# A token tile kept aside and paired with one of a later batch, with other sums for the last softmax

## The chip, the cores and the metric

The kernel runs on one core of a Trainium2 chip. Five engines work side by side, each through its own instructions in order: TensorE (PE; its weight loads PEld), VectorE (DVE), ScalarE (ACT), GpSimd (POOL) and SyncE (SP), which here only issues transfers. The metric is the device time of one execution in microseconds.

## What is computed

Attention with normalised queries and keys, and behind it a two-layer network with a leaky ReLU on all tokens:

```python
q_n, k_n = (rmsnorm(q, g_q), rmsnorm(k, g_k))      # q, k, v: (8, 12, 448, 64)
scores = scale * np.matmul(q_n, k_n.transpose(0, 1, 3, 2))
scores = scores - np.max(scores, axis=-1, keepdims=True)
attn = np.exp(scores)
attn = attn / (np.sum(attn, axis=-1, keepdims=True) + 1e-09)
attn_out = np.matmul(attn, v)
x = attn_out.transpose(0, 2, 1, 3).reshape(3584, 768)
h = x @ w_in                                       # (768, 2048)
out = np.maximum(0.01 * h, h) @ w_out              # (2048, 768)
```

## The kernel before

**Units.** The attention is cut into 24 units `u` of four heads; three units make a batch `b`. A unit computes seven score blocks in four steps `d` (1, 2, 2 and 2 blocks, `STEPS`), through two PSUM slots `sT`; ACT turns each block into exponentials `et` (line 214). At `d == 0` the maximum is formed on DVE (`shift_max`, L232 and L234), a matmul spreads it over the partitions (`shift_mm`, L244), and DVE makes the bias `eb` from it; in the same place PE does the last unit's value products (`pv`, L340) and its softmax sums. For units 4 and up the sums are formed in four column tiles (`zcol`, L283, 128x224): Ln and Exp on 224 columns (L300, L305), four transfers that broadcast the result (`rz`, L310, on SP), a copy of the values out of PSUM (L295), and a multiplication on POOL or, for the last unit, on DVE (L320). The first units use `zsum_slot`, `pv`, `zinv` and `xmul` instead: ones matmuls that leave the sums already spread (L265), Ln and Exp on 896 columns (L326, L327), and a multiplication straight out of PSUM (L349).

**The network as filler.** `push(b)` puts batch `b`'s network into a queue of items, each with a cost in microseconds; `fill(u, d, jobs)` takes items out behind every score step, in proportion to the time that is left (weights `WD`), and puts one of the small `jobs` (loads, squares, sums, norms of later units) behind each. Batch `b` is pushed at unit 3b+3, step 3. Work that an item leaves for DVE, ACT or a queue goes to `pend` (`later`) and is put out by `flush` at the start of the next item or at the end of the fill. What is left after the last unit, three items, covers the last softmax; then batch 7 follows alone.

**First layer.** `moe1(b, ft)` makes one block of 128 of the 2048 hidden features for all 448 tokens with six matmuls and a Prelu on ACT into `gt` (L362, L356). Batches 6 and 7 (`late`) use a seven-product scheme instead (`late1`, L564): for a pair of feature blocks `s`, items `(n, s)` are products of 224 columns, six matmuls each, combined by DVE (L577, L612) before the Prelu (L574). Batch 6 does it for two of four pairs (`LATE_HALF`, in which "M" is a plain `moe1`), batch 7 for all. The operands are sums of weights (`win_sum`, L533) and of tokens (`x_sum`, L550).

**Second layer.** `gt` holds 512 token columns of a pair of batches; `col(t)` gives the place of token tile `t` (0 to 6, 128 tokens). Tiles 0 to 2 belong to the even batch; the odd one overwrites columns 64 to 511. A tile alone is four items of eight matmuls of 128x384 (`moe2`, L403). Two tiles together take seven items of eight (`seven`, L444) with operand sums `sa` from `s1` to `s4` on DVE (L425 to L434). In even batches from 2 on, tile 2 goes alone and 0 and 1 together; in odd ones (3, 4) and (5, 6).

**Banks.** Four PSUM banks serve all these products (`aux`). From batch 6's first `late1` item on, `hold` takes all four and a free list hands them out first in, first out; `drop` returns a bank.

Of the kernel before, what the change touches and what calls it, by code (L numbers as in the profile page):

```python
# [18 lines left out]
def kernel(  # L19
# [44 lines left out]
            banks = [psum.tile([P, 512], FP32, tag="aux", bufs=4, name=f"bank{i}") for i in range(4)]  # L64
            held.append(banks)

    def drop(bank):
        if held:
            held[0].append(bank)

    ident16 = cst.tile([P, P], FP16)
    make_identity(nc, ident16)
# [40 lines left out]
    def rows(x, u):  # L113
        b, g = divmod(u, NQ)
        return x[b, QH * g:QH * g + QH].rearrange("(a r) (p t) d -> (r p) a (t d)", r=2, t=NS)

    def load(u, engines=None):
        raw[u] = [raws.tile([P, 2, NS, D], FP32, tag=name, name=name) for name in ("rq", "rk")]
        st[u] = {}
        for t, src, eng in zip(raw[u], (q, k), engines or (nc.sync, nc.sync)):  # L120
            eng.dma_start(t.rearrange("p a t d -> p a (t d)"), rows(src, u))
# [12 lines left out]
    def buf(u, name):  # L134
        if name not in st[u]:
            shape, dtype, bufs = SHAPES[name]
            st[u][name] = prep_p.tile(shape, dtype, tag=name[:2] if bufs == 3 and name != "qkT" else name, bufs=bufs, name=name)
        return st[u][name]

    BOTH = (0, 1)  # L140
# [171 lines left out]
    def xmul_sb(u):  # L312
        xmul_pool(u, nc.vector)
# [44 lines left out]
    def moe1(b, ft):  # L358
        xt = xts[b]
        hps = aux([P, 512], FP32, "hps")  # L360
        for kt in range(KT):
            nc.tensor.matmul(hps[:, 0:S], win16[:, kt // 2, kt % 2, ts(ft, P)], xt[:, kt // 2, kt % 2],  # L362
                             start=(kt == 0), stop=(kt == KT - 1))
        prelu(b, gt[:, ft, 64 * (b % 2):64 * (b % 2) + S], hps[:, 0:S])
        drop(hps)

    def moe1_part(b, banks, k0, k1):
        for ft in range(2):
# [46 lines left out]
    def weight_sum(n, x):  # L415
# [2 lines left out]
                (wblock(1, 1), wblock(0, 1)), (wblock(1, 0), tw[:, 1]))[n]  # L418
        nc.vector.tensor_tensor(tw[:, n, x], a[:, x], b[:, x], op=ALU.subtract)

    def gblock(t, j):
        return gt[:, HF * j:HF * j + HF, ds(col(t), P)]

    def s1(tt, x=slice(0, 8)):
# [14 lines left out]
    def seven(pair, tt, nxt=None, last=False):  # L439
        g = {}  # L440

        def mm(bank, a, b, first):
            for f in range(HF):
                nc.tensor.matmul(bank[:, 0:HC], a[:, f], b[:, f], start=(first and f == 0), stop=(f == HF - 1), skip_group_check=not first)  # L444

        def bank(name):
            g[name] = aux([P, 512], FP32, name)
            return g[name]

        def add(dst, src, name):  # L450
            nc.vector.tensor_tensor(dst, g[name][:, 0:HC], src, op=ALU.add)

        def put(i, c):
            store(pair, tt[i], g["o"][i], c, last)

        def i0():
            flush()
            g["o"] = (out_tile(), out_tile())
            mm(bank("ma"), gblock(tt[0], 0), wblock(0, 0), True)
            later(lambda: nc.vector.tensor_copy(g["o"][1][:, L], g["ma"][:, 0:HC]))  # L460

        def i1():
            flush()
            mm(bank("mb"), sa[:, 1], tw[:, 1], True)
            later(lambda: add(g["o"][1][:, L], g["o"][1][:, L], "mb"))
            later(lambda: drop(g["mb"]))

        def i2():
            flush()
            mm(g["ma"], gblock(tt[0], 1), wblock(1, 0), False)  # L470
            later(lambda: nc.scalar.copy(g["o"][0][:, L], g["ma"][:, 0:HC]))
            later(lambda: drop(g["ma"]))
            if last:
                later(put, 0, L)

        def i3():
            flush()
            mm(bank("mc"), sa[:, 0], tw[:, 0], True)
            later(lambda: add(g["o"][1][:, R], g["o"][1][:, L], "mc"))
            if nxt:  # L480
                later(s1, nxt)

        def i4():
            flush()
            mm(bank("md"), sa[:, 2], tw[:, 2], True)
            later(lambda: add(g["o"][1][:, R], g["o"][1][:, R], "md"))
            if last:
                later(put, 1, R)

        def i5():  # L490
            flush()
            mm(g["mc"], sa[:, 3], wblock(1, 1), False)
            if nxt:
                later(s2, nxt)
            later(lambda: add(g["o"][0][:, R], g["o"][1][:, L], "mc"))
            later(lambda: drop(g["mc"]))
            later(put, 0, R if last else LR)
            if nxt:
                later(s3, nxt)
                later(s4, nxt)  # L500

        def i6():
# [35 lines left out]

    def x_tiles():
        if not xs:  # L540
            two = [prep_p.tile([P, 2, HK, HX], FP16, tag="sq", bufs=3, name="xs") for i in range(2)]
            for n in range(1, 5):
                xs[n] = two[n // 3][:, (n - 1) % 2].rearrange("p k (t x) -> p k t x", t=NS)

# [7 lines left out]
    def late1(b, tail, after):  # L552
# [36 lines left out]
        def start():  # L589
            hold()  # L590
            if tail:
                for i in range(2):
                    drop(slot()[:, 0])
            for name in ("u", "v"):
                if name not in tmp:
                    tmp[name] = raws.tile([P, 2, S], FP32, tag="rq" if name == "u" else "rk", name=name)

        def item(n, s):
            flush()
# [28 lines left out]
            for fn in after.get((n, s), ()):  # L628
                pend.append(fn)

        return item

    LATE_ALL = ((1, 0), (2, 0), (7, 0), (1, 1), (6, 0), (7, 1), (1, 2), (5, 0), (4, 0), (6, 1), (3, 0), (2, 1), (7, 2), (5, 1),
                (4, 1), (6, 2), (3, 1), (1, 3), (7, 3), (5, 2), (4, 2), (6, 3), (3, 2), (2, 2), (5, 3), (4, 3), (2, 3), (3, 3))
# [1 line left out]
                 (2, 3), (5, 3), (4, 3), "M", (3, 3))  # L636

    queue = []

    def also(fn, *more):  # L640
        def both():
# [5 lines left out]
    def push(b):  # L647
        pair, odd = divmod(b, 2)
        fast = b > 0
        order = [f // 2 + HF * (f % 2) for f in range(FT)] if odd else range(FT)  # L650
        items = [(1.13, lambda ft=ft: (flush(), moe1(b, ft))) for ft in order]
        half = [(slice(0, 4)), (slice(4, 8))]
        late = b >= LATE
# [1 line left out]
        if late:  # L655
            if odd:
                tt = (3, 4)
                for ns, f in (((1, 3), s1), ((4, 2), s2), ((3, 2), s3), ((5, 3), s4)):
                    after[ns] = [lambda f=f: f(tt, half[0])]
                after[3, 3] = [lambda f=f: f(tt, half[1]) for f in (s1, s2)]  # L660
            else:
                after[6, 2] = [lambda: win_sum(1, 0, (raws, "rq", 3))]
                after[1, 3] = [lambda: win_sum(2, 0, (raws, "rk", 3))]
                after[5, 2] = [lambda: win_sum(4, 0, (prep_p, "n16", 1))]
            item = late1(b, odd, after)
            fts = [0, 8, 1, 9, 2, 10, 3, 11]
            items = []
            for w in (LATE_ALL if odd else LATE_HALF):
                if w == "M":
                    items.append((1.13, lambda ft=fts.pop(0): (flush(), moe1(b, ft))))  # L670
                else:
                    items.append((0.575, lambda w=w: item(*w)))
        if odd:
            tt, tn = (3, 4), (5, 6)
            items += [(1.31, fn) for fn in seven(pair, tt, tn)]
            for n, x, fs in ((len(items) - 7, 1, (s3, s4)),) if late else ((8, 0, (s1, s2)), (10, 0, (s3, s4)), (FT - 1, 1, (s1, s2)), (FT, 1, (s3, s4))):
# [3 lines left out]
        else:  # L680
            tiles = (2,) if fast else (0, 1, 2)
            std = [lambda t=t, h=h, p=p: moe2(pair, t, h, p) for t in tiles for h in range(2) for p in range(2)]
            if fast:
                tt = (0, 1)
                std[0] = also(std[0], lambda: later(s1, tt), *[lambda: later(win_sum, 3, 0)] * late)
                std[1] = also(std[1], lambda: later(s2, tt))
                std[2] = also(std[2], lambda: later(s3, tt), lambda: later(s4, tt))
                std += seven(pair, tt)
# [55 lines left out]
    with tc.manual_schedule():  # L744
# [182 lines left out]
        for u in range(3, NU):  # L927
            for d in range(4):
# [67 lines left out]
                if d == 2 and 6 <= u < 8:  # L996
                    job(xmul_sb, u - 1)
                if u == NU - 2 and d == 0:
                    for n, tile_ in ((1, (raws, "rq", 3)), (2, (raws, "rk", 3)), (3, None), (4, (prep_p, "sq", 3))):
                        job(win_sum, n, 1, tile_)  # L1000
                    for n in (3, 1, 2, 4):
                        job(x_sum, LATE, n)
# [1 line left out]
                    for ti in range(2):  # L1004
                        job(prep_sq, u + 3, ALL, (ti,))
                fill(u, d, jobs)
        zcol(NU - 1)
        zcol_ln(NU - 1)
        zcol_inv(NU - 1)
        pv_slot(NU - 1)  # L1010
        pv_out(NU - 1)
        for i, fns in enumerate(([lambda: xmul_sb(NU - 1)], [lambda n=n: x_sum(B - 1, n) for n in (3, 1)], [lambda n=n: x_sum(B - 1, n) for n in (2, 4)])):
            c, fn = queue[i]
            queue[i] = (c, also(fn, *[lambda f=f: later(f) for f in fns]))
        push(B - 1)
        while queue:
            queue.pop(0)[1]()
# [29 lines left out]
```

## Time and profile before

| | us |
|---|---|
| median of 3 runs | 422.75 |
| lowest and highest | 422.69, 425.65 |
| the profiled execution | 425.65 |
| its span, first to last instruction | 423.8 |
| PE busy, weight loads | 404.8, 223.4 |
| ACT busy | 303.6 |
| DVE busy | 272.4 |
| POOL busy | 82.9 |
| chain that ended last: PE, ACT, DVE | 71%, 14%, 8% |

The spans are those of one profiled execution, which is also the slowest of the three runs. PE's busy time is that of its pipeline: a stall shorter than a matmul's flight doesn't show as idle. Units 5 to 21 take between 13.0 and 16.8 us each, unit 22 takes 18.8 and unit 23 17.6 us (from one maximum to the next, and to the last unit's sums). The last unit's sums start at 374.66 us, batch 7's first layer at 380.81 and its second layer at 401.04.

### The profile page before, as it was taken

Reading aid. Unit: us, or ns where it says so; the run is one execution under the profiler, and the core shown is the slowest. Engines: PE = TensorE matmul, PEld = TensorE weight load, DVE = VectorE, ACT = ScalarE, POOL = GpSimd, SP = SyncE. Lnnn points to the kernel's source line nnn. Section 1 sums busy time; section 2 is a strip of 40 time slices with the busy share of each in tenths; the row PEclk is TensorE's granted clock in tenths of the full one; section 3 lists DMA queues with packets and bytes.
Section 4 is the critical chain, followed back from the end, with each engine's and each line's share of the span. In section 5 each row is a group of like instructions: output and inputs, shape, how many; then the busy total and the mean of one; then the engine's idle time right before and its main releaser. Section 6 shows DMA issues by size and latency. Waiting matters only on the chain.

```text
span 423.8 us, 9575 instructions
## 1 busy us (share of the span) xinstructions
PE 404.8 (96%) x3959; PEld 223.4 (53%) x3959; DVE 272.4 (64%) x439; ACT 303.6 (72%) x475; POOL 82.9 (20%) x75
## 2 busy tenths in 40 slices
PE   7787999999999999999999999999999999998996
PEld 6454454544445544555445545555445557557963
DVE  5888674886668736665458736565448779416762
ACT  5999877778886599777887689767887476633600
POOL 1967432200020211210210211210220110010000
PEclk9999999999999999999999999999999999998999
DMA  7999997899555885668564896678532550232013
GB/s 265 216 251 252 240 251 110 210 159 209 142 152 97 216 230 88 162 180 175 142 153 78 208 208 132 159 179 172 153 67 47 137 142 2 48 76 77 2 47 104
DMA packets 72527, 62.88 MB, mean 148 GB/s; under 512 B 36388, under 2 KB 67620, under 8 KB 72484
## 3 DMA queue, kind: packets, MB, share of 16 engines
q1 hardware_dynamic: 61888, 50.08, 46.3%
q0 software_dynamic: 10272, 11.80, 17.8%
q8 instruction: 31, 0.51, 0.5%
q10 hardware_dynamic: 324, 0.39, 0.3%
q14 instruction: 12, 0.10, 0.1%
HBM read 45.61 MB, written 11.01 MB: 134 GB/s over the span
## 4 chain that ended last, share of the span: by engine, by line
PE 71%; ACT 14%; DVE 8%; issue 3%; DMA 2%; SPq 1%; DVEq 0%; ACTq 0%
PE hps L362 23%; ACT et L214 8%; PE sT L195 7%; PE sT L340 5%; PE ma L444 5%; PE md L444 5%; PE bank L564 4%; PE mc L444 4%; PE bank L444 4%; PE op L403 3%; PE zc L283 3%; PE mb L444 3%; DVE n L167 2%; ACT gt L356 2%; PE sT L444 2%
## 5 line engine op out<-in xcount | busy, mean ns | idle before, releaser
L214 ACT ACTIVATE et<-sT,eb 128x896 f16<-128x896 f32 x166 | 159.6, 1011 | 18.6 <-PE sT L195 16.8
L362 PE MATMUL hps<-xt,win 128*128 128x448 f16 x600 | 120.8, 353 | 0.2 <-DVE xt L349 0.2
L362 PEld LDWEIGHTS <-win 128*128 128x128 f16 x612 | 56.8, 98 | 58.2 <-issue 9.7
L320 POOL TENSOR_TENSOR xt<-x,rz 128x896 f16<-128x896 f32 x16 | 33.3, 2084 | 153.6 <-DMA rz<-zs 127.4
L167 DVE TENSOR_TENSOR n<-rq,rinv 128x896 f16<-128x896 f32 (+2 forms) x25 | 30.5, 1221 | 47.3 <-ACT rinv L161 44.5
L356 ACT ACTIVATE gt<-hps 128x448 f16<-128x448 f32 x100 | 54.1, 557 | 6.0 <-PE hps L362 5.4
L195 PE MATMUL sT<-qkT 64*64 64x448 f16 x664 | 52.4, 363 | 4.4 <-ACT et L214 3.4
L155 DVE TENSOR_REDUCE ssq<-sq 128x14 f32<-128x896 f32 (+2 forms) x49 | 50.4, 1058 | 1.1 <-ACT sq L144 1.1
L444 PEld LDWEIGHTS <-sa 128*128 128x128 f16 x352 | 32.8, 98 | 26.3 <-issue 6.1
L295 ACT COPY x<-sT 128x896 f32<-128x896 f32 x20 | 18.1, 906 | 38.0 <-DVE sT L245 37.3
L124 POOL DMA_DIRECT2D vt<-in_v_dram x24 | 18.2, 757 | 110.2 <-PE sT L340 102.8
L195 PEld LDWEIGHTS <-qkT 64*64 64x64 f16 x672 | 15.4, 104 | 37.8 <-issue 34.4
L444 PEld LDWEIGHTS <-gt 128*128 128x128 f16 x264 | 25.2, 98 | 18.9 <-issue 2.4
L340 PE MATMUL sT<-et,vt 64*64 64x448 f16 x560 | 30.0, 350 | 0.3
L403 PE MATMUL op<-wout,gt 128*128 128x384 f16 x160 | 28.4, 327 | 0.0
L340 PEld LDWEIGHTS <-vt 64*64 64x64 f16 x672 | 20.6, 107 | 11.4 <-issue 1.9
L232 DVE TENSOR_REDUCE sT<-sT 128x1 f32<-128x896 f32 x22 | 24.0, 1093 | 3.3 <-PE sT L195 3.3
L167 DVE TENSOR_TENSOR n<-rk,rinv 128x896 f16<-128x896 f32 (+2 forms) x26 | 26.1, 1010 | 0.0
L403 PEld LDWEIGHTS <-gt 128*128 128x128 f16 x192 | 17.6, 98 | 14.3 <-issue 3.0
L444 PE MATMUL ma<-wout,gt 128*128 128x384 f16 x128 | 23.5, 326 | 0.0
L425 DVE TENSOR_TENSOR sa<-gt 128x512 f16<-128x512 f16 (+1 forms) x15 | 8.2, 544 | 18.5 <-ACT gt L356 13.8
L144 ACT ACTIVATE sq<-rq 128x896 f32<-128x896 f32 (+2 forms) x18 | 16.3, 913 | 1.2 <-DMA rq<-in_q_dram 1.2
(133 smaller groups left out, 514.7 us busy)
## 6 DMA issues: line engine op xcount, KB each, us to landing
rq<-in_q_dram SPq DMA_DIRECT2D x24, 448.0 KB, 3.9
rk<-in_k_dram SPq DMA_DIRECT2D x24, 448.0 KB, 5.4
out_dram<-ost SPq DMA_DIRECT2D x52, 192.0 KB, 3.5
rz<-zs SPq DMA_DIRECT2D x80, 112.0 KB, 2.3
vt<-in_v_dram POOLq DMA_DIRECT2D x24, 224.0 KB, 5.7
win<-in_moe_w_in_dram POOLq DMA_DIRECT2D x8, 384.0 KB, 15.3
wout<-in_moe_w_out_dram POOLq DMA_DIRECT2D x2, 1536.0 KB, 28.8
out_dram<-ost SPq DMA_DIRECT2D x4, 96.0 KB, 2.2
```

What stands on the lines that cost most here:

```text
L124: nc.gpsimd.dma_start(vts[u % NV].rearrange("p a t d -> p a (t d)"), rows(v, u))
L155: nc.vector.tensor_reduce(buf(u, "ssq")[:, ti, :, c[0]:c[1]], buf(u, f"sq{ti}")[:, :, c[0]:c[1]], axis=AXL.X, op=ALU.add)
L167: nc.vector.tensor_tensor(buf(u, "n16")[:, ti, c[0]:c[1]].rearrange("p s a d -> p a s d"), src[:, :, c[0]:c[1]], buf(u, "rinv")[:, ti, :, ...
L195: nc.tensor.matmul(banks[a][64 * r:64 * r + 64, 0:S].rearrange("p (t x) -> p t x", t=NS), kT(u, r, a, t), qT(u, r, a), start=True, stop=True)
L214: nc.scalar.activation(s["et"][:, t], sT[:, :, 0:S], AF.Exp, bias=s["eb"], scale=1.0)
L232: nc.vector.tensor_reduce(s["spare"][:, 511:512], sT[:, :, 0:S], axis=AXL.XY, op=ALU.max)
L320: eng.tensor_tensor(xts[b][:, g], s["x32"], s["rz"], op=ALU.mult)
L340: nc.tensor.matmul(s["pv"][r][64 * a:64 * a + 64, 0:S], vts[u % NV][64 * r:64 * r + 64, a, t], s["et"][64 * r:64 * r + 64, t, a], start=(t ...
L356: nc.scalar.activation(dst, src, AF.Prelu, bias=0.0, scale=1.0, alpha=0.01)
L362: nc.tensor.matmul(hps[:, 0:S], win16[:, kt // 2, kt % 2, ts(ft, P)], xt[:, kt // 2, kt % 2], start=(kt == 0), stop=(kt == KT - 1))
L403: nc.tensor.matmul(op2[:, 0:HC], gt[:, ft, ds(col(t), P)], wout16[:, ft, ds(HC * half, HC)], start=(ft == 0), stop=(ft == FT - 1))
L444: nc.tensor.matmul(bank[:, 0:HC], a[:, f], b[:, f], start=(first and f == 0), stop=(f == HF - 1), skip_group_check=not first)
```

## The change

- Batch 4 (`KEEP`) no longer does tile 2. Behind its first pair item a transfer on SP copies the tile's columns out of `gt` into `kept`; batch 6 does its own tile 2 and the kept one together with seven half products, ahead of the pair (0, 1). The kept tile's output is stored there.
- Batch 4's feature blocks are made in the order of the odd batches, and its operand sums are formed in two halves, at items 8, 10, 15 and 16.
- Batch 6's `late1` items are those of `mid`: product 2 is accumulated onto product 1's bank, product 6 onto a copy of product 1 in a second bank, and the Prelus read PSUM where they can. The banks are held from its first "M" on.
- The last unit uses `zsum_slot`, `pv`, `zinv` and `xmul`; the token sums of batch 7 are put behind the first two left items.
- Scratch tiles move: the squares use two buffers from unit 9 on, and the third holds `kept` and later a tile of batch 7.

```diff
-    def drop(bank):
+    full = []
+    def drop(bank, whole=False):
         if held:
             held[0].append(bank)
+            full[:] = [x for x in full if x is not bank] + [bank] * whole
+    def written():
+        for i, x in enumerate(held[0]):
+            if any(x is y for y in full):
+                return held[0].pop(i)
...
+    def keep(pair):
+        kept["pair"] = pair
+        kept["g"] = ring(prep_p, "sq", True, [P, FT, P], FP16, "kept")
+        nc.sync.dma_start(kept["g"], gt[:, :, ds(col(2), P)])
...
+        def mid(n, s):
+            flush()
+            hold()
+            if n == 1:
+                mm(get(1, s), 1, s, x_b(b, 0, 0), True)
+                later(lambda: g.__setitem__((6, s), written()))
+                later(lambda: nc.vector.tensor_copy(g[6, s][:, 0:S], g[1, s][:, 0:S]))
+            elif n == 7:
+                mm(get(7, s), 7, s, xs[3], True)
+                g["w", s] = opool.tile([P, S], FP32, tag="ost", name="w")
+                later(lambda: nc.vector.tensor_copy(g["w", s], g[7, s][:, 0:S]))
+            elif n == 2:
+                mm(g[1, s], 2, s, x_b(b, 1, 0), False)
+                later(lambda: out_(s, 0, 0, g[1, s][:, 0:S]))
+                later(lambda: drop(g[1, s], True))
+            elif n == 6:
+                mm(g[6, s], 6, s, xs[2], False)
+                later(lambda: vadd(g[7, s][:, 0:S], g[6, s], g["w", s]))
+            elif n == 5:
+                mm(g[6, s], 5, s, xs[1], False)
+                later(lambda: vadd(g["w", s], g[6, s], g["w", s]))
+                later(lambda: out_(s, 1, 1, g["w", s]))
+            elif n == 4:
+                mm(g[7, s], 4, s, xs[4], False)
+                later(lambda: out_(s, 1, 0, g[7, s][:, 0:S]))
+                later(lambda: drop(g[7, s], True))
+            else:
+                mm(g[6, s], 3, s, x_b(b, 1, 1), False)
+                later(lambda: out_(s, 0, 1, g[6, s][:, 0:S]))
+                later(lambda: drop(g[6, s], True))
+            for fn in after.get((n, s), ()):
+                pend.append(fn)
...
-        order = [f // 2 + HF * (f % 2) for f in range(FT)] if odd else range(FT)
+        order = [f // 2 + HF * (f % 2) for f in range(FT)] if odd or b == KEEP else range(FT)
...
-        if odd:
+        if b == KEEP:
+            tt = (0, 1)
+            items += [(1.31, fn) for fn in seven(pair, tt)]
+            for n, x, fs in ((8, 0, (s1, s2)), (10, 0, (s3, s4)), (FT - 1, 1, (s1, s2)), (FT, 1, (s3, s4))):
+                c, fn = items[n]
+                items[n] = (c, also(fn, *[lambda f=f, x=x: later(f, tt, half[x]) for f in fs], *[lambda: later(keep, pair)] * (n == FT)))
+        elif late and not odd:
+            tt, tn = (2, "kept"), (0, 1)
+            items += [(1.31, fn) for fn in seven(pair, tt, tn)]
+            for n, x, fs in ((len(items) - 9, 0, (s1, s2)), (len(items) - 8, 1, (s1, s2)), (len(items) - 7, 0, (s3, s4)), (len(items) - 7, 1, (s3, s4))):
...
+            items[len(items) - 8] = (c, also(fn, lambda: later(win_sum, 3, 0)))
+            items += [(1.31, fn) for fn in seven(pair, tn)]
+        elif odd:
...
-        zcol(NU - 1)
-        zcol_ln(NU - 1)
-        zcol_inv(NU - 1)
-        pv_slot(NU - 1)
-        pv_out(NU - 1)
-        for i, fns in enumerate(([lambda: xmul_sb(NU - 1)], [lambda n=n: x_sum(B - 1, n) for n in (3, 1)], [lambda n=n: x_sum(B - 1, n) for n in (2, 4)])):
+        zsum_slot(NU - 1)
+        pv(NU - 1)
+        zinv(NU - 1)
+        xmul(NU - 1)
+        for i, ns in enumerate(((3, 1), (2, 4))):
             c, fn = queue[i]
-            queue[i] = (c, also(fn, *[lambda f=f: later(f) for f in fns]))
+            queue[i] = (c, also(fn, *[lambda n=n: later(x_sum, B - 1, n) for n in ns]))
```

More of the change, by code (lines that the diff above doesn't have):

```diff
@@ L65, in hold @@
             held.append(banks)
-    def drop(bank):
+    full = []
+    def drop(bank, whole=False):
         if held:
             held[0].append(bank)
+            full[:] = [x for x in full if x is not bank] + [bank] * whole
[3 more added lines that the diff above has]
+                return held[0].pop(i)
+        raise RuntimeError("no bank whose 448 columns TensorE has written")
     ident16 = cst.tile([P, P], FP16)
@@ L115, in rows, with ring @@
         return x[b, QH * g:QH * g + QH].rearrange("(a r) (p t) d -> (r p) a (t d)", r=2, t=NS)
+    def ring(pool, tag, third, shape, dtype, name):
+        return pool.tile(shape, dtype, tag=tag + "ab"[third], bufs=1 if third else 2, name=name)
     def load(u, engines=None):
@@ L136, in buf @@
             shape, dtype, bufs = SHAPES[name]
-            st[u][name] = prep_p.tile(shape, dtype, tag=name[:2] if bufs == 3 and name != "qkT" else name, bufs=bufs, name=name)
+            if name in ("sq0", "sq1"):
+                third = u < 9 and (2 * u + int(name[2])) % 3 == 2
+                st[u][name] = ring(prep_p, "sq", third, [P, 2, NS + third, D], dtype, name)[:, :, 0:NS]
+            else:
+                st[u][name] = prep_p.tile(shape, dtype, tag=name, bufs=bufs, name=name)
         return st[u][name]
@@ L364, in moe1 @@
         prelu(b, gt[:, ft, 64 * (b % 2):64 * (b % 2) + S], hps[:, 0:S])
-        drop(hps)
+        drop(hps, True)
     def moe1_part(b, banks, k0, k1):
@@ L419, in weight_sum @@
         nc.vector.tensor_tensor(tw[:, n, x], a[:, x], b[:, x], op=ALU.subtract)
+    kept = {}
+    def keep(pair):
+        kept["pair"] = pair
+        kept["g"] = ring(prep_p, "sq", True, [P, FT, P], FP16, "kept")
+        nc.sync.dma_start(kept["g"], gt[:, :, ds(col(2), P)])
     def gblock(t, j):
+        if t == "kept":
+            return kept["g"][:, HF * j:HF * j + HF]
         return gt[:, HF * j:HF * j + HF, ds(col(t), P)]
@@ L453, in put @@
         def put(i, c):
-            store(pair, tt[i], g["o"][i], c, last)
+            if tt[i] == "kept":
+                store(kept["pair"], 2, g["o"][i], c, last)
+            else:
+                store(pair, tt[i], g["o"][i], c, last)
         def i0():
@@ L540, in x_tiles @@
         if not xs:
-            two = [prep_p.tile([P, 2, HK, HX], FP16, tag="sq", bufs=3, name="xs") for i in range(2)]
+            two = [ring(prep_p, "sq", False, [P, 2, HK, HX], FP16, "xs") for i in range(2)]
             for n in range(1, 5):
@@ L593, in start @@
                     drop(slot()[:, 0])
-            for name in ("u", "v"):
-                if name not in tmp:
-                    tmp[name] = raws.tile([P, 2, S], FP32, tag="rq" if name == "u" else "rk", name=name)
+            tmp["u"] = ring(prep_p, "sq", True, [P, 2, S], FP32, "u")
+            tmp["v"] = raws.tile([P, 2, S], FP32, tag="rk", name="v")
         def item(n, s):
@@ L629, in item @@
                 pend.append(fn)
-        return item
+        def mid(n, s):
[24 more added lines that the diff above has]
+                later(lambda: drop(g[7, s], True))
+            else:
+                mm(g[6, s], 3, s, x_b(b, 1, 1), False)
[3 more added lines that the diff above has]
+                pend.append(fn)
+        return item if tail else mid
     LATE_ALL = ((1, 0), (2, 0), (7, 0), (1, 1), (6, 0), (7, 1), (1, 2), (5, 0), (4, 0), (6, 1), (3, 0), (2, 1), (7, 2), (5, 1),
@@ L638 @@
     queue = []
+    KEEP = 4
     def also(fn, *more):
@@ L663, in push @@
                 after[1, 3] = [lambda: win_sum(2, 0, (raws, "rk", 3))]
-                after[5, 2] = [lambda: win_sum(4, 0, (prep_p, "n16", 1))]
+                after[5, 2] = [lambda: win_sum(4, 0, (raws, "rq", 3))]
             item = late1(b, odd, after)
@@ L669, in push @@
                 if w == "M":
-                    items.append((1.13, lambda ft=fts.pop(0): (flush(), moe1(b, ft))))
+                    items.append((1.13, lambda ft=fts.pop(0): (flush(), hold(), moe1(b, ft))))
                 else:
                     items.append((0.575, lambda w=w: item(*w)))
-        if odd:
+        if b == KEEP:
[8 more added lines that the diff above has]
+            for n, x, fs in ((len(items) - 9, 0, (s1, s2)), (len(items) - 8, 1, (s1, s2)), (len(items) - 7, 0, (s3, s4)), (len(items) - 7, 1, (s3, s4))):
+                c, fn = items[n]
+                items[n] = (c, also(fn, *[lambda f=f, x=x: later(f, tt, half[x]) for f in fs]))
+            c, fn = items[len(items) - 8]
+            items[len(items) - 8] = (c, also(fn, lambda: later(win_sum, 3, 0)))
+            items += [(1.31, fn) for fn in seven(pair, tn)]
+        elif odd:
             tt, tn = (3, 4), (5, 6)
@@ L684, in push @@
                 tt = (0, 1)
-                std[0] = also(std[0], lambda: later(s1, tt), *[lambda: later(win_sum, 3, 0)] * late)
+                std[0] = also(std[0], lambda: later(s1, tt))
                 std[1] = also(std[1], lambda: later(s2, tt))
@@ L998 @@
                 if u == NU - 2 and d == 0:
-                    for n, tile_ in ((1, (raws, "rq", 3)), (2, (raws, "rk", 3)), (3, None), (4, (prep_p, "sq", 3))):
+                    for n, tile_ in ((1, (raws, "rq", 3)), (2, (raws, "rk", 3)), (3, None), (4, (prep_p, "n16", 1))):
                         job(win_sum, n, 1, tile_)
```

## The prediction

> **What bounds the kernel now.** I read the busy shares first, then the windows of the stages that the change touches, then the timelines of their seams.
>
> ```profile
> span 423.8 us, 9575 instructions
> ...
> PE 404.8 (96%) x3959; PEld 223.4 (53%) x3959; DVE 272.4 (64%) x439; ACT 303.6 (72%) x475; POOL 82.9 (20%) x75
> ```
>
> TensorE bounds the whole. The next windows (span, then busy of PE, PEld, DVE, ACT, POOL, then granted clock) are units 16, 17, 18 and 19, which consume batch 4's items, then units 22 and 23, the last item stretch, and batch 7's first layer.
>
> ```profile
> 241.74:257.20 15.46, 15.46 (x144) 7.46 (x140) 7.52 (x12) 13.12 (x22) 2.83 (x2) 1.00 0.84 201
> 257.20:272.83 15.63, 15.53 (x160) 7.61 (x156) 8.05 (x13) 14.02 (x24) 2.83 (x2) 1.00 0.62 140
> 272.83:288.64 15.81, 15.81 (x158) 8.49 (x153) 11.12 (x20) 11.36 (x17) 2.83 (x2) 1.00 0.68 154
> 288.64:305.46 16.82, 16.82 (x156) 8.05 (x152) 7.80 (x14) 13.90 (x25) 2.83 (x2) 1.00 0.77 176
> 338.24:357.06 18.82, 18.82 (x202) 12.18 (x198) 15.59 (x27) 13.23 (x21) 2.08 (x1) 1.00 0.39 89
> 357.06:374.66 17.60, 17.12 (x166) 9.60 (x154) 8.05 (x15) 10.77 (x16) 2.08 (x1) 1.00 0.21 49
> ...
> 381.60:401.04 19.44, 17.45 (x163) 16.46 (x161) 14.60 (x27) 9.26 (x18) 0.00 (x0) 0.91 0.15 41
> ```
>
> Units 16 to 19 have next to no idle PE, but ACT stands only 1.6 to 4.5 us behind it, so PE work taken out there pays only until ACT is late. In units 22 and 23 both are freer: work added there is paid in full. Batch 7's stretch is different: its clock is below 1. The PE timeline there (last bracket: idle before, and what ended it):
>
> ```profile
> 380.81 0.83 PE L564 MATMUL bank<-xt,win 128*128 128x224 f16 x7
> 383.24 0.64 PE L564 MATMUL bank<-xt,win 128*128 128x224 f16 x5 [1.59 <-DVE xt L320]
> 384.12 0.73 PE L564 MATMUL bank<-xs,win 128*128 128x224 f16 x6 [0.24 <-DVE xs L550]
> 385.00 1.22 PE L564 MATMUL bank<-xt,win 128*128 128x224 f16 x6 [0.15 <-DVE ost L451]
> 386.02 1.33 PE L564 MATMUL bank<-xs,ws 128*128 128x224 f16 x6
> ```
>
> PE waits 1.59 us for the last unit's normalisation, whose four broadcasts go through a transfer, and then six matmuls take 1.33 instead of 0.74 us. Windows cut at that seam, and one early in the kernel, show why:
>
> ```profile
> 381.60:385.00 3.40, 1.42 (x12) 1.05 (x11) 2.91 (x6) 0.52 (x1) 0.00 (x0) 1.00 0.05 13
> 385.00:388.40 3.40, 3.40 (x19) 2.80 (x19) 2.58 (x5) 1.00 (x2) 0.00 (x0) 0.51 0.81 219
> ...
> 33.50:36.90 3.40, 2.24 (x34) 1.35 (x35) 3.34 (x6) 2.94 (x4) 2.38 (x3) 1.00 1.12 244
> ```
>
> After 3.4 us with PE busy 42%, the clock is halved for the next 3.4 us; 66% busy left it whole.
>
> **Part 1, batch 4 loses its plain tile.** Thirty-two 128x384 matmuls go; eight take 1.30 us in the chain, so 4 x 1.30 = 5.2 us of PE. The filler spreads a shorter list, and its arithmetic (cost 0.5, weights WD) gives which items fall where. Unit 16 holds two first-layer items fewer (2 x 1.16 us = 2.3); but its second step has one item, so the second pair of scores waits for exponentials (pairs take 1.90 us): 0.6 back, gain 1.7. Unit 17 now holds nine first-layer items instead of seven and two plain quarters, and ends on the last two. That seam is new. The half sums of blocks 4 to 7 are put behind the last item and stand on DVE ahead of unit 18's maximum. They need the last Prelu, which on ACT stands behind two exponentials, a Prelu and a square. The same ACT order at the seam 16/17 (256.39 gt, 256.81 sq, 257.65 gt) ends 1.4 us after the next scores start; two half sums (0.42 each), the maximum (1.09) and the diagonal (0.29) follow. The shift matmul comes 3.7 us after the scores, where PE is there after 2.4 (256.69 to 259.12): 1.3 us idle, less 0.5 us saved earlier: unit 17 loses 0.8. Queued behind the waiting DVE are only that maximum and the shift, but PE and ACT wait for these. Unit 18: seven half products and one first-layer item against nine items, 1.4 us, less 0.4 for a one-item step: 1.0. Unit 19 has one first-layer item less: 1.2, with ACT at 13.9 of 16.8. Part 1: 1.7 - 0.8 + 1.0 + 1.2, a gain of **3.1 us**; its ends are 5.2 (ACT and DVE never late) and 1.0 (ACT late in units 16 and 18 too).
>
> The transfer that keeps the tile (512 KB in 256-byte rows) goes on SP behind four rz broadcasts and ahead of unit 22's load. No such transfer is in the trace; the nearest are rz (112 KB, 2.3 us to landing) and rk (448 KB, 5.4 us). Batch 5's first Prelu, which overwrites the columns, comes some 13 us after it, the load behind it is needed 27 us later, and the tile itself 60 us later: nothing. Were this cover gone, PE would wait its 5 us once. Squares on two buffers after unit 9: a square at 257.65 is summed by 265.2, the next is written at 271.97; 6.8 us of cover, nothing.
>
> **Part 2, batch 6 gets seven half products for four plain quarters.** 24 matmuls more, 3 x 1.30 = 3.9 us, in units 22 and 23. Its `mid` form accumulates product 2 onto product 1's bank and product 6 onto a copy in a second bank: two DVE additions go (0.62 each, off the path), but a unit of four banks is now full. I followed the free list by hand. Product (2,2) waits for the copy of (1,2): 0.2 + 0.62 us against 0.58 us of (7,2): 0.3. At (7,3) the list holds only the bank of (4,2), just finished. So (7,3) waits for that bank's Prelu; ACT does the Prelu of (5,2) before it; that waits for its DVE addition; and that stands behind the copy of (1,3) and a 0.95 us weight sum. The copy itself goes into the bank of the preceding first-layer item and waits for its Prelu, which follows two exponentials. From the scores' start: exponentials until 2.3, Prelu 2.8, copy 3.4, weight sum 4.3, addition 4.9, Prelus 5.5 and 6.0, product (7,3) 6.1, where PE is there at 3.5: **2.6 us** idle, with unit 22's remaining scores queued behind. Another 0.3 for (5,3). In unit 23:
>
> ```profile
> 359.42 0.91 ACT L295 COPY x<-sT 128x896 f32<-128x896 f32 x1 [1.67 <-DVE sT L245]
> 360.23 1.01 ACT L214 ACTIVATE et<-sT,eb 128x896 f16<-128x896 f32 x1
> 361.13 0.36 ACT L300 ACTIVATE zs<-bank 128x224 f32<-128x224 f32 x1
> 361.37 0.59 ACT L574 ACTIVATE gt<-v 128x448 f16<-128x448 f32 x1
> ```
>
> The Prelu of (3,3) cannot start before 361.4, 2.6 us after the shift. The first half product now follows (3,3) at once and needs its block 6 after 1.6 us; it gets it at 3.2: 1.6 us idle, where before, with three items ahead, PE lost 0.6 there. Part 2: 3.9 + 0.3 + 2.6 + 0.3 + 1.0 = 8.1, less 0.2 us of gaps in the old order, **7.9 us**; ends 3.9 and 8.4.
>
> **Part 3, the last unit's sums without the transfer.** 28 ones matmuls of 448 columns (1.32 us, row L265) for 28 of 224 (0.79): 0.5 more on PE. Then Ln and Exp of 128x896 (0.90 and 0.95, rows L326, L327) and two DVE multiplications (0.62 each, row L349) end 4.7 us after the sums start; PE still has products and three items until 6.7. So batch 7 starts without a wait. Its first seven products took 8.15 us (380.81 to 388.96) where six-matmul groups go at 0.575: 4.1 us lost, gone, less 0.3 for its DVE queue. Part 3: 0.5 - 4.1 + 0.3, a gain of **3.3 us**; ends 3.6 and 1.6 (if the halved clock was this execution's alone).
>
> **The clock.** The 2.6 us gap of part 2 can leave a 3.4 us window 24% busy, below the 42% that halved the clock; the loss is 3.4/2 = 1.7 us. If a window's edge falls inside the gap it may not. Between 0 and 1.7 I take 1.2, for the gap is longer than the row's.
>
> The Trainium skill, "TensorE: Matmul & The Clock Gate", section "Why this matters for your kernels", asks only for no idle gaps above about 3 us; by it a gap of 2.6 us costs no clock and the sum would be 1.2 us lower. This trace halved the clock after gaps of 1.59, 0.24 and 0.15 us, so I go by the row.
>
> **Sum.** -3.1 + 7.9 - 3.3 + 1.2 = +2.7 us. The profiled execution took 425.65 us (span 423.8 and 1.85 around it), 2.9 above the median; I add the difference to the median: 422.75 + 2.7, about 425.5 us.
>
> **Rivals.** *PE work alone decides* (faster): no bank wait, no seam wait. Then -5.2 + 3.9 - 3.6 = -4.9, 417.9 us. For it: PE is busy 96% and the change leaves eight matmuls fewer and removes the 1.59 us wait; against it: the free list and ACT's order above. Chance 0.20. *The clock is halved again and again* (slower): the gaps of 1.5 us in unit 18, 2.6 in unit 22 and 1.6 in unit 23 each cost 1.7 us: 1.5 + 3 x 1.7 = +6.6, 429.4 us. It decides if a window that is 53% busy is enough, which lies between the rows of 42% and 66%. Chance 0.22. *The kept tile comes late*, so that the change does not do what it says: the transfer holds up batch 5's first Prelu for 5 us, 430 us; against it the 13 us of cover. Chance 0.03. *Forecast*: 0.55, between 421.5 (bank wait absent, part 1 as summed) and 428.
>
> **How the numbers follow.** Within 1% (418.5 to 427.0, about what a measurement of this kernel can tell from no change) lies most of the forecast and the upper half of the fast rival: 0.63. Faster: half of the fast rival, 0.10. Slower: the two slow rivals and the forecast's upper edge: 0.27. The range for 8 in 10 cuts half of the fast rival and the ends of the slow ones: 418.8 to 429.5.
>
> **What would show it.** Right: in the window of units 16 to 19 some 3 us less; a PE wait of over 1 us for DVE at unit 18's shift; a PE wait of about 2.6 us for ACT on a bank in unit 22; one of 1.6 us at the first half product of unit 23; no wait at batch 7's second product and clock 1.00 there. Wrong: units 22 and 23 only 4 us longer, or units 16 to 19 shorter by the full 5.2.

## The result, and the profile after

The changed kernel takes 429.78 us (median of 6 runs, 427.93 to 430.82); beside it the one before took 423.31. The ratio is 1.014 (95% interval 1.0107 to 1.0172): 1.4% slower, some 6 us. Its profiled execution took 428.84 us. The page's head:

```profile
span 427.0 us, 9574 instructions
...
PE 404.2 (95%) x3951; PEld 222.6 (52%) x3951; DVE 275.6 (65%) x452; ACT 303.8 (71%) x475; POOL 83.0 (19%) x75
```

Eight matmuls fewer and less PE time, and yet a longer span: over the whole, time was added not as work but as waits. The windows of the same stages (units 16 to 19, then 22 and 23, then batch 7's first layer; columns as before) tell where:

```profile
240.78:254.68 13.90, 13.53 (x136) 6.48 (x132) 7.59 (x12) 12.30 (x21) 2.83 (x2) 1.00 0.90 221
254.68:271.15 16.47, 16.47 (x196) 7.97 (x188) 8.57 (x15) 15.60 (x26) 3.16 (x3) 1.00 0.65 144
271.15:286.78 15.63, 13.21 (x108) 6.76 (x104) 11.87 (x19) 10.94 (x17) 2.51 (x2) 1.00 0.67 159
286.78:302.54 15.76, 15.76 (x154) 7.47 (x150) 7.73 (x13) 12.92 (x23) 2.83 (x2) 1.00 0.76 180
...
335.32:360.75 25.43, 22.83 (x216) 14.66 (x212) 15.92 (x28) 15.13 (x25) 2.08 (x1) 0.93 0.28 66
360.75:381.29 20.54, 19.12 (x178) 10.35 (x170) 11.40 (x23) 9.48 (x14) 2.09 (x1) 1.00 0.26 61
...
387.97:404.07 16.10, 16.10 (x170) 16.10 (x168) 12.03 (x23) 9.27 (x18) 0.00 (x0) 1.00 0.19 50
```

| stage | before, profiled | before, second execution (e1) | after |
|---|---|---|---|
| units 16 to 19 | 63.7 | 63.9 | 61.8 |
| unit 22 | 18.8 | 18.8 | 25.4 |
| unit 23, to its sums | 17.6 | 17.6 | 20.5 |
| last sums to the end | 49.1 | 47.4 | 45.7 |
| span | 423.8 | 421.4 | 427.0 |

Batch 4's stage gives back 2 us and the end 1.7 to 3.4; unit 22 costs 6.6 and unit 23 2.9. Batch 7's first layer now runs without a gap, 28 x 0.575 us. What PE waited for in the changed kernel (us in total, times, longest):

```profile
PE bank L592 <- ACT gt L602: 2.4, 1, 2.4
...
PE bank L469 <- ACT gt L602: 1.6, 2, 1.4
PE sT L260 <- DVE dg L250: 1.3, 1, 1.3
...
PE md L469 <- DVE ost L476: 1.0, 1, 1.0
```

These are the bank wait of unit 22, the first half product of unit 23, the shift at the seam 17/18, and one that the prediction did not have, in unit 18. The timeline of the bank wait (start, duration, instruction, idle before) shows the whole chain:

```profile
350.23 0.63 DVE L664 COPY bank<-bank 128x448 f32<-128x448 f32 x1 [1.21 <-ACT gt L372]
350.77 0.95 DVE L561 TENSOR_TENSOR ws<-ws,win 128x1536 f16<-128x1536 f16 x1
351.63 0.62 DVE L605 TENSOR_TENSOR w<-bank,w 128x448 f32<-128x448 f32 x1
...
352.29 0.58 ACT L602 ACTIVATE gt<-w 128x448 f16<-128x448 f32 x1 [2.09 <-DVE w L605]
352.77 0.53 ACT L602 ACTIVATE gt<-bank 128x448 f16<-128x448 f32 x1
353.35 0.73 PE L592 MATMUL bank<-xs,win 128*128 128x224 f16 x6 [2.39 <-ACT gt L602]
```

The copy waits for the plain item's Prelu, the weight sum goes ahead of the addition, ACT does one Prelu and then the one that frees the bank. Windows from the wait on show the second price:

```profile
350.88:354.29 3.41, 1.02 (x15) 0.62 (x13) 2.36 (x4) 1.01 (x2) 0.00 (x0) 1.00 0.00 0
354.29:357.70 3.41, 3.41 (x25) 2.48 (x18) 1.14 (x2) 2.34 (x3) 0.00 (x0) 0.52 0.00 0
```

PE is busy 30% of 3.4 us, and the next 3.4 us run at half clock.

### The profile page after: what moved, and what is told of

The parts are those of the page before. It is cut to its first block, busy times and chain, and to the rows that moved or that the text cites. A ratio compares the mean times of both kernels' runs of the same rounds, so it can differ in the third digit from the quotient of the medians.

```text
span 427.0 us, 9574 instructions
## 1 busy us (share of the span) xinstructions
PE 404.2 (95%) x3951; PEld 222.6 (52%) x3951; DVE 275.6 (65%) x452; ACT 303.8 (71%) x475; POOL 83.0 (19%) x75
## 4 chain that ended last, share of the span: by engine, by line
PE 76%; ACT 12%; DVE 7%; issue 2%; DMA 1%; SPq 0%; DVEq 0%; ACTq 0%
PE hps L378 24%; ACT et L230 8%; PE sT L211 7%; PE bank L469 7%; PE sT L356 5%; PE ma L469 5%; PE md L469 5%; PE bank L592 4%; PE mc L469 4%; PE zc L299 3%; PE mb L469 3%; PE op L419 2%; DVE n L183 2%; PE bank L378 2%; PE sT L469 2%
## 5 line engine op out<-in xcount | busy, mean ns | idle before, releaser
L378 PE MATMUL hps<-xt,win 128*128 128x448 f16 x564 | 114.0, 353 | 0.2 <-DVE xt L365 0.2
L372 ACT ACTIVATE gt<-hps 128x448 f16<-128x448 f32 x94 | 50.8, 556 | 6.1 <-PE hps L378 5.6
L469 PEld LDWEIGHTS <-sa 128*128 128x128 f16 x384 | 35.7, 98 | 28.9 <-issue 7.0
L311 ACT COPY x<-sT 128x896 f32<-128x896 f32 x19 | 17.2, 906 | 37.9 <-DVE sT L261 37.9
L469 PEld LDWEIGHTS <-gt 128*128 128x128 f16 x280 | 26.6, 98 | 22.4 <-issue 3.4
L356 PE MATMUL sT<-et,vt 64*64 64x448 f16 x532 | 28.4, 349 | 0.2
L248 DVE TENSOR_REDUCE sT<-sT 128x1 f32<-128x896 f32 x22 | 24.1, 1095 | 5.1 <-PE sT L211 5.1
L419 PE MATMUL op<-wout,gt 128*128 128x384 f16 x128 | 22.7, 327 | 0.0
L160 ACT ACTIVATE sq<-rk 128x896 f32<-128x896 f32 x17 | 16.3, 959 | 0.7 <-DMA rk<-in_k_dram 0.7
```

Source lines behind the costliest of these rows:

```text
L160: nc.scalar.activation(buf(u, f"sq{ti}")[:, :, c[0]:c[1]], raw[u][ti][:, :, c[0]:c[1]], AF.Square)
L248: nc.vector.tensor_reduce(s["spare"][:, 511:512], sT[:, :, 0:S], axis=AXL.XY, op=ALU.max)
L356: nc.tensor.matmul(s["pv"][r][64 * a:64 * a + 64, 0:S], vts[u % NV][64 * r:64 * r + 64, a, t], s["et"][64 * r:64 * r + 64, t, a], start=(t ...
L372: nc.scalar.activation(dst, src, AF.Prelu, bias=0.0, scale=1.0, alpha=0.01)
L419: nc.tensor.matmul(op2[:, 0:HC], gt[:, ft, ds(col(t), P)], wout16[:, ft, ds(HC * half, HC)], start=(ft == 0), stop=(ft == FT - 1))
```

## The experiments

All times are medians beside runs of before on the same chip; before lay between 423.2 and 423.8 us in every set. Half a per cent is 2 us, and intervals are some 0.2% each way, 0.8 us; smaller claims rest on the profiles. The ratio is that to before on the same chip. The sets ran on different chips, so two kernels of different sets are compared more safely by their ratios than by their medians; such a difference is known to some 1.5 us each way.

**e1, before again**, unchanged.

> The unchanged kernel of before, for the clock of its single runs. Theory W (waits): the difference of the medians (6.5 us) is made of waits and items, and every run of before has its clock halved once in batch 7's first layer, as the profiled one had: mean clock 0.995 in all runs. Theory C (clock): the profiled run of before, 2.9 us above the median, was an exception; the runs near 422.7 us have a mean clock of 0.998 or more and spans near 421 us, while those of the changed kernel are at 0.987 to 0.995, that is one to three stretches of 3.4 us at half clock.

423.33 us, ratio 0.9996 (0.9984 to 1.0009). Its profiled execution has mean clock 1.0 and a span of 421.4; windows at the same seam of batch 7's first layer:

```profile
380.40:383.80 3.40, 2.00 (x18) 1.51 (x16) 2.88 (x6) 0.53 (x1) 0.00 (x0) 1.00 0.05 12
383.80:387.20 3.40, 3.06 (x31) 2.90 (x31) 3.12 (x6) 1.53 (x3) 0.00 (x0) 1.00 0.82 221
```

With 59% busy the clock stayed whole; the wait for the broadcasts was 1.0 us, not 1.59. Runs of before have mean clocks from 0.990 to 1.0, but no run of e1 reached 425 us, and of the 79 runs of before on record only two did; so the profiled execution that the prediction priced was an unlucky one. Theory C holds in that; its "0.998 or more" does not: low mean clocks occur near 422.7 us too. A mean clock doesn't say where the clock was halved: in six profiles (e2, e6, e8, e9, e10, e11) it was halved somewhere between 10 and 19 us, where other engines set most of the pace. What that cost isn't clear: the scores of unit 2 start between 26.8 and 27.7 us there, and between 26.7 and 27.3 in the other eight. In three of the six (e6, e8, e11) it was halved again between 36 and 40 us, and unit 2 took 11.8 us instead of 10.9.

**e2, part 3 alone.**

```diff
-        zcol(NU - 1)
-        zcol_ln(NU - 1)
-        zcol_inv(NU - 1)
-        pv_slot(NU - 1)
-        pv_out(NU - 1)
+        zsum_slot(NU - 1)
+        pv(NU - 1)
+        zinv(NU - 1)
+        xmul(NU - 1)
```

> Before, with part 3 of the change alone (the last unit by zsum_slot, pv, zinv and xmul). Theory W: the 1.59 us wait and the halved clock of batch 7's first layer both go in every run: 0.5 - 4.1 + 0.3 = -3.3 us, about 419.9 us. Theory C: most runs of before had no halved clock to lose, so only the wait goes: -3.3 + 1.7 = -1.6 us, about 421.6 us. Both: no PE wait over 0.3 us at batch 7's second product.

421.45 us, ratio 0.9957 (0.9942 to 0.9971): 1.8 us faster, theory C's figure, and no wait at batch 7's second product. This part of the change is a gain.

**e3, part 3 undone in the changed kernel.**

> The changed kernel with the last unit's sums of before (four column tiles and the transfer): part 3 undone. Theory W: +3.3 to +3.6 us, about 433 us. Theory C: +1.6 us, about 431.4 us, and a clock that is not lower than the changed kernel's own. The PE wait of about 1.6 us at batch 7's second product comes back.

430.09 us, ratio 1.0153 (1.0134 to 1.0172): 0.3 us over the changed kernel, which the intervals don't separate; neither theory. In its profile the wait for the broadcasts is 0.27 us: SP put out the four of them in 2.5 us, against 3.3 (e1) and 3.8 (before). In the profiles the stretch from the last sums to the end is 46.7 us against the changed kernel's 45.7, so part 3 is worth about 1.0 us here by the profiles and less by the times. Why SP is slower with them in before wasn't tried.

**e4, batch 6's items reordered.**

```diff
-(1, 3), (5, 2), (4, 2), (7, 3), (3, 2), (6, 3), (2, 3), (5, 3), (4, 3), "M", (3, 3))
+(1, 3), (5, 2), (4, 2), (2, 3), (3, 2), (7, 3), (6, 3), (5, 3), (4, 3), "M", (3, 3))
-                after[1, 3] = [lambda: win_sum(2, 0, (raws, "rk", 3))]
-                after[5, 2] = [lambda: win_sum(4, 0, (raws, "rq", 3))]
+                after[6, 3] = [lambda: win_sum(2, 0, (raws, "rk", 3))]
+                after[5, 3] = [lambda: win_sum(4, 0, (raws, "rq", 3))]
```

> The changed kernel with batch 6's items in another order, (2,3) and (3,2) between (4,2) and (7,3), and the two weight sums of DVE put behind (6,3) and (5,3): product (7,3) no longer asks for the bank just finished. Theory of the prediction (bank wait of 2.39 us, and a halved clock behind it): the wait falls to about 0.4 us and the clock stays 1.00 in unit 22: -2.0 - 1.7 = -3.7 us, about 426 us. Rival (the halved clock in unit 22 comes from something else, or the wait moves to the next product): -2.0 us or less, about 428 us.

426.46 us, ratio 1.0078 (1.0056 to 1.0100): 3.3 us less by the medians, 2.6 by the ratios. The bank wait is gone, one of 0.9 us for a DVE addition is left, the clock is 1.00 in unit 22. 1.5 us of waits are gone, so 1.1 to 1.8 us are more than the wait.

**e5, the seam 17/18.**

```diff
+                    if u == 17:
+                        jobs = [lambda: None, lambda: None]
                     for ti in range(2):
                         job(prep_sq, u + 3, ALL, (ti,))
```

> The changed kernel; at the last step of unit 17 the two squares on ACT stand behind both Prelus instead of between and behind them. Theory of the prediction (the shift of unit 18 waits for two half sums, these for the last Prelu, this for a square): the Prelu ends 0.85 us earlier, PE's wait for the diagonal falls from 1.32 to about 0.5 us, 0.8 us less in unit 17. Rival (the maximum is late for another reason): the wait stays at 1.3 us and the time is the same.

PE's wait at the shift fell from 1.32 to 0.49 us and unit 17 from 16.47 to 15.64, as expected. The time fell by more, to 427.16 us (1.0092; 1.0072 to 1.0111): 2.6 us by the medians, 2.0 by the ratios.

**e6, (3,3) ahead of the last plain item.**

```diff
-                 (2, 3), (5, 3), (4, 3), "M", (3, 3))
+                 (2, 3), (5, 3), (4, 3), (3, 3), "M")
```

> The changed kernel; in batch 6's list (3,3) comes ahead of the last plain first-layer item. Theory of the prediction (the first half product of the kept pair waits for the Prelu of (3,3), which stands behind the value copy and an exponential): PE's wait of 1.42 us for ACT there goes, 1.4 us less. Rival (the wait moves: the third half product needs the plain item's Prelu, which now stands in the same place on ACT): 0.5 us less or nothing.

The wait of 1.42 us at the first half product is gone and unit 23 has no other; to its sums it is 1.2 us shorter (19.3). The time is 427.62 us (1.0104; 1.0086 to 1.0123), 2.2 us less by the medians and 1.5 by the ratios. In this execution units 16 and 21, which the edit doesn't touch, are 0.8 and 0.6 us longer: a norm beside POOL's multiplication takes 2.97 and 2.23 us, the matter of e7.

**e7, unit 18 without POOL's multiplication.**

```diff
-                if d == 1 and narrow(u - 1) and not 5 <= u < 8 and u < NU - 1:
+                if d == 1 and narrow(u - 1) and not 5 <= u < 8 and u < NU - 1 and u != 18:
+                if u == 18 and d == 2:
+                    job(xmul_sb, u - 1)
```

> The changed kernel; in unit 18 the multiplication of unit 17's values is done by DVE behind its norms instead of by POOL beside them. In the changed kernel a norm took 2.86 us there instead of 1.09 and PE waited 1.0 us for the addition behind it. Theory P (POOL beside DVE slows the norm): the norm takes 1.1 us, the wait goes, about 1.0 us less in unit 18. Rival T (the 512 KB transfer of the kept tile, under way at the time, slows it): the norm stays near 2.8 us, the wait stays.

The changed kernel's timeline in unit 18:

```profile
280.20 2.08 POOL L336 TENSOR_TENSOR xt<-x,rz 128x896 f16<-128x896 f32 x1 [8.62 <-ACT uu L176]
...
280.37 2.86 DVE L183 TENSOR_TENSOR n<-rq,rinv 128x896 f16<-128x896 f32 x1 [0.23 <-ACT rinv L177]
...
283.15 0.54 DVE L476 TENSOR_TENSOR ost<-md,ost 128x384 f32<-128x384 f32 x1
...
283.75 1.46 PE L469 MATMUL md<-tw,gt 128*128 128x384 f16 x8 [1.00 <-DVE ost L476]
```

The same norm in e7, with the kept tile's transfer put out as before:

```profile
280.22 1.09 DVE L183 TENSOR_TENSOR n<-rq,rinv 128x896 f16<-128x896 f32 x1 [0.24 <-ACT rinv L177]
```

Theory P holds: the wait is gone and unit 18 falls from 15.63 to 14.47 us. The time is 428.17 us (1.0109; 1.0085 to 1.0134), 1.6 us less by the medians and 1.3 by the ratios.

**e8, all four together.**

> The changed kernel with the reordering, the seam, the swap and the multiplication on DVE together. If the waits are separate and add up: 3.3 + 0.8 + 1.4 + 1.0 = 6.5 us below the changed kernel, about 423.3 us, the time of before. If one wait only uncovers the next: 425 us or more.

423.55 us, ratio 1.0000 (0.9988 to 1.0011): 6.2 us below the changed kernel, and the time of before. The four causes make up the net loss. But only the sum agrees: alone they gave 3.3 + 2.6 + 2.2 + 1.6 = 9.7 us by the medians, and 2.6 + 2.0 + 1.5 + 1.3 = 7.4 by the ratios, against 5.9 for all four.

**e9, the changed kernel again**, since by the medians e5 to e7 gave more than the waits they removed (0.8, 1.4 and 1.0).

> The changed kernel again, for the clock of its single runs. It was timed at 429.78 us, with mean clocks from 0.987 to 0.995; kernels that differ from it in 0.8 to 1.4 us of waits were then 2.2 to 2.6 us below it, with clocks from 0.986 to 0.998. Theory C (the rest was stretches at half clock, which come and go from run to run): now about 428.0 to 428.5 us, and within the runs a lower clock goes with a longer time. Rival (the mended waits are worth more than their length): 429.8 us again.

429.85 us (1.0140; 1.0112 to 1.0167): the time repeats, and theory C's 428.0 to 428.5 fails. Its profile again shows half clock behind the bank wait. The mean clock of its twelve runs, those of the first measurement included, lies between 0.986 and 0.995; the six of e5 have 0.990 to 0.998.

**e10, a version that beats both?** Before with e2's and e6's edits.

> Before with the new sums for the last unit and, in batch 6's list, (3,3) ahead of the last plain item: the 0.5 us wait of the first plain quarter for the Prelu of (3,3) goes as well. If both parts add up: 421.45 - 0.5, about 421.0 us. If the wait only moves: 421.4 us.

421.46 us, ratio 0.9945 (0.9925 to 0.9964). Its profile has no wait over 0.2 us from unit 16 on, so the swap does what it should, but e2 is no slower within the interval. Both beat before and after.

**e11, the kept tile's transfer twice.**

> The changed kernel with the transfer of the kept tile issued twice, the second behind the first's landing on SP's queue. Theory of the prediction (the transfer is hidden; only unit 22's load stands behind it): the same time as the changed kernel, within 0.3 us. Rival (the transfer costs through SP or through the transfer engines): 1 us or more on top, in unit 18 or 19.

429.77 us (1.0142; 1.0116 to 1.0167), the changed kernel's own time, though SP was held 4.8 us by the two instead of 0.6. In its profile unit 19 is 1.2 us longer, since there a norm falls beside POOL's multiplication (2.83 us) and PE waits 0.7 us more at the next shift; unit 20 is 0.5 us shorter. So the second transfer may shift the broadcasts, which isn't shown; what a single one costs is below what these runs can tell.

**e12, PE kept busy in the bank wait.**

```diff
             elif n == 7:
+                if s == 3:
+                    warm(36, slot()[:, 0])
                 mm(get(7, s), 7, s, xs[3], True)
```

> The changed kernel with 36 matmuls of 128x128 on a free score slot, results unused, ahead of product (7,3): some 2.1 us of PE work in the 2.39 us in which PE waits there. Nothing else becomes earlier. Theory C (the clock is halved behind this wait in most runs of the changed kernel, as in both of its profiled executions): the clock stays 1.00 in unit 22, 1.3 to 2 us less, about 428.0 us. Rival (the halved clock there is rare, or costs nothing in the end): the same time, 429.8 us, or slightly more.

428.13 us (1.0103; 1.0084 to 1.0123): 36 matmuls more, and 1.7 us less by the medians, 1.6 by the ratios. The windows of the wait and of what follows:

```profile
350.90:354.30 3.40, 3.02 (x48) 2.69 (x50) 2.34 (x5) 1.01 (x2) 0.00 (x0) 1.00 0.00 0
354.30:357.70 3.40, 3.25 (x37) 2.77 (x30) 1.49 (x3) 2.77 (x4) 0.00 (x0) 1.00 0.02 5
```

Unit 22 takes 24.1 us, as in the profiles in which the wait is there and the clock stayed whole, against 25.4: the product comes no earlier, but the clock stays whole. So the halved clock behind this wait is worth 1.3 us in the profile, and about 1.6 us in the times, which are known less well.

## Why the prediction was right, and where it was off

It said slower, by 2.7 us; it is slower, by about 6. The direction was right and the size was not: the prediction gave 0.63 to a time within 1% of before and 0.27 to slower, and 429.78 us lies above the 428 at which its forecast ended. The mechanisms that it named came as described, one was missing (unit 18), and four terms were off, all on the same side.

- **Part 1, a gain of 3.1 us: 2.0 to 2.1.** Unit 16 gave 1.6 (predicted 1.7), unit 17 lost 0.8 (0.8), unit 19 gave 1.1 (1.2). Unit 18 gave 0.2 instead of 1.0. The step "seven half products and one first-layer item against nine items, 1.4 us, less 0.4 for a one-item step" had the items right and left out what a shifted timeline lays side by side: unit 18's norm now falls on POOL's multiplication, takes 2.86 us, and PE waits 1.0 us for the addition queued behind it. e7 shows it.
- **Part 2, 7.9 us: 8.2 without the clock.** Unit 22 grew by 6.6, of which 1.3 is the halved clock (the same bank wait without it leaves unit 22 at 24.1 us, in e3, e5 and e7), and unit 23 by 2.9. The bank wait was 2.39 us (2.6 predicted), the wait for the copy 0.2 (0.3), that at the first half product 1.42 (1.6), each with the releaser named; a wait of (5,3), 0.3 predicted, doesn't show. e4 and e6 remove the two long ones. The matmuls (3.9) and these waits, less the 0.5 that PE waited in unit 23 before, make 7.4; the other 0.8 isn't traced, so that 7.9 came so near 8.2 is partly luck.
- **Part 3, a gain of 3.3 us: 1.7 to 1.8** (e1 and e2; undone in the changed kernel, 0.3 to 1.0, e3). The term was taken from an execution that was itself disturbed. "4.1 us lost" for batch 7's first seven products held 1.7 us of half clock and a longer transfer; the typical execution has neither (e1). The sum should have used the lower end, 1.6, that the text gave for just this case; the hint was the 2.9 us by which the profiled execution stood above the median. The sum was then added to the median, which doesn't contain the half clock that part 3 was credited with removing.
- **The clock, 1.2 us: 1.3 in the profile, about 1.6 by e12.** The row was the better guide: in both profiles of the changed kernel the gap of 2.4 us was followed by half clock. In five others it was not, which the prediction's "If a window's edge falls inside the gap it may not" allows (below). The page "TensorE: Matmul & The Clock Gate" of the Trainium skill, section "Why this matters for your kernels", asks for no idle gaps above about 3 us, so by it this gap would have been free; the window of 30% busy and e12 say otherwise for this kernel.
- **The transfer, the squares on two buffers, the DVE additions saved: nothing.** e11 bears this out for the transfer, within its interval; the other two weren't tried alone.

With the measured terms, -2.1 + 8.2 - 1.7 + 1.3 = 5.7 us, beside 1.4% of 423.3, 5.9 us. Against the disturbed profile alone the span grew by only 3.2 us, near the predicted 2.7; that is luck, for the stages ahead of unit 16, in which no term of the sum lies, happened to take 1.0 us less. The rival "PE work alone decides" falls: PE's busy time fell by 0.6 us while the span grew. "The clock is halved again and again" came close in size but not in kind: in the changed kernel's two profiles the clock was halved behind the bank wait, and not behind the gaps of 1.32 and 1.42 us.

**The excess of e5 to e7.** By the medians each alone gave 0.6 to 1.8 us more than its wait (2.6 against 0.8, 2.2 against 1.4, 1.6 against 1.0). By the ratios, which leave the chips out, they gave 2.0, 1.5 and 1.3 us, and the rest is within what such a difference is known to.

**When the wait halves the clock.** In the profiles of e3, e5, e6, e7 and e11 the bank wait of 2.39 us is there and the clock behind it is whole; in both profiles of the changed kernel it is halved. The granted clock shows what differs. In each execution the stretches at half clock start on one grid of 3.41 us: at 354.42 and 426.10 us in the changed kernel, 21 steps apart; at 12.66, 36.56 and 425.68 us in e11, 7 and 114 steps apart. In the changed kernel and in e9 the wait lies almost whole in one step of this grid, of which PE fills 31% and 41%. In e5, e6, e7 and e11 an edge of the grid cuts the wait, and the emptier step is 53% to 64% full. One step of e11 at half clock, and the two between which its wait is split:

```profile
36.56:39.97 3.41, 3.41 (x40) 2.16 (x43) 2.89 (x4) 2.17 (x3) 3.41 (x3) 0.50 1.11 248
...
350.58:353.99 3.41, 2.27 (x21) 1.92 (x20) 2.20 (x4) 1.50 (x3) 0.00 (x0) 1.00 0.00 0
353.99:357.41 3.42, 2.18 (x25) 1.63 (x25) 1.64 (x3) 2.08 (x4) 0.00 (x0) 1.00 0.00 0
```

In e3 no stretch at half clock shows where the grid lies. So, by two profiles against four, the same wait halves the clock or not by where it falls on the grid.

**Left open:** how many executions of the changed kernel lose the clock there. The profiled executions of e3, e5 and e7, with the clock whole behind the wait, are each the fastest of their six, by 0.9 to 1.7 us; that suggests that most others lose it, and doesn't show it.

## What to carry to other kernels

Work that is moved from a stage where it is nearly hidden to a stage where it is paid must be summed by stage: 5.2 us of matmuls taken out gave 2.1, and 3.9 us put in elsewhere cost 8.2. When a product is kept in its bank to save an addition, follow the free list to the next product: a bank handed out right after its last reader was queued makes PE wait for everything that stands ahead of that reader on ACT and DVE. And price a stall from a typical execution: look at how the profiled one stands to the median before taking a term from it.

## What the runs showed of the hardware

- A DVE multiplication of 128x896 with both operands in SBUF took 2.86 us when it started 0.17 us behind a POOL multiplication of 2.08 us, and 1.09 us without it: it ended 0.95 us after POOL's end, as if it had stood still until then; so did the slow norms of e4 in unit 21 and of e6 in units 16 and 21. "SBUF — State Buffer" of the Trainium skill, section "Summary: rules for kernel authors", says this: a DVE operation with two SBUF inputs and a GpSimd operation that reads SBUF exclude each other for a whole instruction. The numbers agree, to the 0.14 us between 0.95 and 1.09. In unit 18 it shows in all eight profiles of the changed kernel and its variants in which POOL does that multiplication (2.84 to 2.86 us). Elsewhere it differs by execution: in unit 16 of e6 (2.97 us), in unit 19 of e11 (2.83), in unit 21 of e4 (2.30) and e6 (2.23). In the changed kernel 14 of POOL's 16 such starts waited for the broadcasts, which may be why.
- Windows of 3.4 us with PE busy 30% and 42% were followed by 3.4 us at half clock; windows with 59% and 66% were not. In between the share alone doesn't decide: 53% was followed by half clock in e6 (32.61 us) and not in e5 (347.84 us). Filling a wait with 36 matmuls whose results are unused made the kernel some 1.6 us faster.
- The stretches at half clock lie on a grid of 3.41 us whose place differs from execution to execution. A wait of 2.39 us halved the clock in the two profiles in which it lay within one step of the grid, and left it whole in the four in which an edge cut it and in one in which the grid's place isn't known.
